# Four combinations of a weight matrix, made in sixteen slices between matmul pieces instead of in one stretch

## The chip, the cores and the metric

The kernel runs on one core of a Trainium2 chip. The time is what the device takes for one execution, in microseconds (us), as the median of the runs shown. The core's engines work side by side, each through its own list of instructions in order, and wait for each other through semaphores: TensorE (PE in the profile, its weight loads PEld), VectorE (DVE), ScalarE (ACT), GpSimd (POOL) and SyncE (SP), which here only starts transfers.

## The reference

A delta-rule attention over 4 batches of 8 heads (768 steps, heads of 48), and a feed-forward block on its output. All is float32.

```python
for t in range(S):
    y[:, :, t] = q_t @ state
    v_old = state applied to k_t                       # k normalized per head
    state = state + beta_t * outer(k_t, v_t - v_old)
x = y as (3072 tokens, 384)
h = x @ w_in                                           # w_in 384 x 2048
g = h * sigmoid(1.702 * h)
out = g @ w_out                                        # w_out 2048 x 384
```

## The kernel before, in words

**Units and pairs.** The sequence is cut into six chunks of 128 steps. A chunk of one batch is a unit, so there are 24 units, numbered 0 to 23, four per chunk. Two neighbouring units (256 tokens) are a pair, and the feed-forward block is done by pairs.

**The attention work of a unit.** The key tile KN of a unit is normalized (`normalize`, lines 296 to 310) in three steps: POOL squares it (`ksq`, line 300); DVE sums the squares (`ssq`) and POOL takes a power of them (`rn`, line 305); DVE adds a small number and takes the reciprocal, and POOL multiplies KN by it (line 309). Then PE transposes KN (`psT`), forms its Gram matrix (`psG`), and a transfer through DRAM puts the diagonal blocks into the tile NT. For every two units DVE inverts these blocks by some twenty pairs of a product `P` and a reduction (`invert`, line 427). Separately POOL masks a unit's score tile M by a select (line 578). There are seven KN buffers, KN0 to KN6; a buffer's next load is started from POOL's own list (line 94), once PE has read the buffer for the last time.

**The feed-forward block.** `hidden` (line 678) makes one pair's `x @ w_in` in sixteen pieces of three matmuls (`ph`; each matmul is two records in the profile), and ScalarE applies the activation into the tiles `gT`. For the first two pairs, `both_written` and `written` multiply `gT` by w_out as it stands (tile `po`). From the third pair on, `seven` (line 725) does the product over 2 x 2 blocks with seven products in place of eight. These need four combinations of the blocks W11, W12, W21, W22 of w_out, made once by `combined` (line 720): T1 = W12 - W11, T2 = W22 - T1, T3 = W22 - W12 (written over W12), T4 = W21 - T2. T1, T2 and T4 lie side by side in the scratch tile TW, 1536 columns each. The second pair's `gT` tiles for the upper half of w_out's rows lie in TW too, in columns 0 to 2047 (`late_g`), and columns 2048 and up hold a mask M and older tiles. So TW may be written only after PE's last products of the second pair that read those columns.

**The order.** `woven(n)` (line 910) writes out the work of step n: the attention steps of units n-1, n and n+1, the normalization of unit n+5, the inversion, and between them `spend`, which takes feed-forward pieces from a queue by a cost budget (`take`, line 833). `follow(n)` appends the next pair's `hidden` and `seven` to that queue. PE, DVE and ACT instructions go through a wrapper that keeps the written order. The POOL instructions of these steps (`ksq`, `rn`, the multiplication of KN, the select, the additions `add`, the loads of KN) don't: a scheduler places them in POOL's list. In this kernel the four additions of `combined` are emitted at the end of the second pair's `written`, by the small generator in the change below.

Of the kernel before, what the change touches and what calls it, by code (L numbers as in the profile page):

```python
# [18 lines left out]
def kernel(  # L19
# [32 lines left out]
    HB = 2  # L52
    NTH = HB * C
    FQ = 4
    GB = 6
    HF, HM = FC // 2, DM // 2
# [18 lines left out]
    units = [(c, b) for c in range(NC) for b in range(B)]  # L75
# [15 lines left out]
    def load(n, pairs, dma=nc.sync.dma_start):  # L91
        c, b = units[n]
        for dst, src in pairs:
            dma(  # L94
                out=place(dst, n)[:, :, 0:D],
                in_=src[b, :, c * C : (c + 1) * C, :].rearrange("h p d -> p h d"),
            )

    def load_values(n, dma=nc.sync.dma_start):
        c, b = units[n]  # L100
        V = io.tile([128, H, D], F32, tag="V", name="V", bufs=4)
        dma(
            out=V, in_=v[b, :, c * C : (c + 1) * C, :].rearrange("h p d -> p h d")
        )
        loaded[n] = V
# [183 lines left out]
    def fill(n):  # L289
        for _ in range(n):  # L290
            next(converting, None)
# [379 lines left out]
    add_, sub_ = ALU.add, ALU.subtract  # L671
    late_g = [TW[:, a : a + FQ * NTH].rearrange("p (f t) -> p f t", f=FQ) for a in (0, 1024)]

    def g_tile():

        return wk.tile([128, FQ, NTH], F32, tag="gT", name="gT", bufs=GB)

    def hidden(xT, gT, t, cost, sums=None, late=False):

        n = t.stop - t.start  # L680
        for f0 in range(0, FC, 2):
            if f0 // FQ == len(gT):
                gT.append(late_g[f0 // FQ - 2] if late and f0 >= FC // 2 else g_tile())
            ph = ps_moe.tile([128, 2, n], F32, tag="moe", name="ph")
            for u in range(2):
                f = f0 + u
                for j in range(KC):
                    pe.matmul(
                        ph[:, u], lhsT=w_in[:, j, f * 128 : (f + 1) * 128], rhs=xT[:, j, t],
                        start=(j == 0), stop=(j == KC - 1),  # L690
                    )
                if u == 0:
                    yield cost
            act.activation(
                gT[f0 // FQ][:, f0 % FQ : f0 % FQ + 2, t], ph, ACT.Gelu_apprx_sigmoid
            )
            if sums is not None and f0 + 2 in (3 * FQ, 4 * FQ):
                k = (f0 + 2) // FQ - 3
                if k == 0:
                    sums.append(g_tile())  # L700
                lo, hi, S1 = gT[k], gT[k + 2], half_of(sums[0], k)
                add(S1, lo[:, :, C:NTH], hi[:, :, C:NTH], add_)
                add(lo[:, :, C:NTH], lo[:, :, 0:C], lo[:, :, C:NTH], sub_)
            yield cost

    def half_of(t, k):

        return t.rearrange("p f (o t) -> p (f o) t", o=2)[:, k * FQ : (k + 1) * FQ]

    def add(o, a, b, op, engine=None):  # L710
        (engine or nc.gpsimd).tensor_tensor(o, a, b, op=op)  # L711
# [7 lines left out]

    def combined():  # L720

        for o, a, b in ((T1, W12, W11), (T2, W22, T1), (T3, W22, W12), (T4, W21, T2)):
            add(o, a, b, sub_)

    def seven(c, b0, gT, sums):

# [69 lines left out]
    def written(c, b0, gT):  # L796

        for i in range(HB):
            b = b0 + i
            po = ps_moe.tile([128, DM], F32, tag="moe", name="po")  # L800
            for f in range(FC):
                pe.matmul(
                    po, lhsT=gT[f // FQ][:, f % FQ, i * C : (i + 1) * C], rhs=w_out[:, f, :],
                    start=(f == 0), stop=(f == FC - 1),
                )
                if f % 2 == 1 and f < FC - 1:
                    yield 1.3
            o = wk.tile([128, DM], F32, tag="o", name="o")
            act.copy(o, po)
            nc.sync.dma_start(out=out[b * S + c * C : b * S + (c + 1) * C, :], in_=o)  # L810
            yield 1.3

    def both_written(c, gT):

        po = [ps_moe.tile([128, DM], F32, tag="moe", name="po") for _ in range(HB)]
        for n, f in enumerate(order):
            while ("out", f - f % 2 if 4 <= f < 8 else f) not in done:
                fill(1)
            fill(3)
            for i in range(HB):  # L820
                pe.matmul(
                    po[i], lhsT=gT[f // FQ][:, f % FQ, i * C : (i + 1) * C], rhs=w_out[:, f, :],
                    start=(n == 0), stop=(n == FC - 1),
                )
            if n < FC - 1:
                yield 1.3
        for i in range(HB):
            o = wk.tile([128, DM], F32, tag="o", name="o")
            act.copy(o, po[i])
            sync(out=out[i * S + c * C : i * S + (c + 1) * C, :], in_=o)  # L830
        yield 1.3
# [11 lines left out]
    def run(work):  # L843
        for _ in work:
            pass
# [5 lines left out]
    steps, xTs, inverting = {}, {}, iter(())  # L851
# [32 lines left out]
    def follow(n):  # L884

        if n + 3 < len(units):
            load(n + 3, ((QP, q),))
        m = n - 1 + len(KN)
        if m < len(units):
            load(m, ((KN, k),), nc.gpsimd.dma_start)  # L890
        if n - 1 + B < len(units):
            load_values(n - 1 + B)
        if n % HB == 0 and n > B:
            h = (n - 1) // HB
            gT, sums = [], []
            queue.append(hidden(xTs[h], gT, slice(0, NTH), 1.3, sums))
            queue.append(seven(*units[h * HB], gT, sums))
            xTs.pop(h)

# [10 lines left out]
    def woven(n, share):  # L910
# [36 lines left out]
        next(new_step(n + 2).scored, None)  # L947
        spend(share / 6)
        follow(n)

    queue = []
# [119 lines left out]
    gTs = [], []  # L1071
# [31 lines left out]
    while ffn:  # L1103
        feed()
    fill(10)
    def last_written():
        yield from written(*units[HB], gTs[1])
        combined()

    queue = [both_written(0, gTs[0]), last_written()]  # L1110
    for n in range(B - 1, len(units) + 1):
        woven(n, 19.5 if n > 6 else 10.4)
    run(take(1e9))
# [31 lines left out]
```

## Time and profile before

| | us |
|---|---|
| median of 3 runs | 823.84 |
| lowest and highest run | 815.86, 824.9 |
| span of the profiled execution | 813.5 |

What an execution takes beside its span isn't in the profile; the lowest run is 2.4 us above the span, the median 10.3.

| engine | busy us | share | instructions |
|---|---|---|---|
| PE | 748.9 | 92% | 8464 |
| DVE | 501.4 | 62% | 1029 |
| POOL | 249.4 | 31% | 210 |
| ACT | 238.5 | 29% | 523 |

| stretch, us from the start of the span | length | PE busy | granted clock of PE |
|---|---|---|---|
| 0 to 120 | 120.0 | 96.9 | 0.73 |
| 120 to 203 | 83.0 | 67.1 | 0.94 |
| 203 to 264 | 61.0 | 51.5 | 0.92 |
| 264 to 296 | 32.0 | 23.3 | 0.89 |
| 296 to 614 | 318.0 | 314.9 | 1.00 |
| 614 to 813.5 | 199.5 | 195.3 | 1.00 |

Times are counted from the start of the span. "Released" or "<-" names what an engine waited for last. The granted clock is the share of its full speed that PE was given. Nearly all instructions carry line 109, which is the wrapper's; they are told apart by their tiles, "out<-in".

### The profile page before, as it was taken

How to read it: one execution, taken by the hardware profiler on the slowest of the kernel's cores; microseconds unless marked ns; L12 is line 12 of the kernel's file. 1: busy time of each engine (PE TensorE's matmuls, PEld its weight loads, DVE VectorE, ACT ScalarE, POOL GpSimd, SP SyncE). 2: the span in 40 equal slices, each digit the busy share in tenths (PEclk: the TensorE clock that was granted, in tenths of full speed). 3: DMA queues.
4: the chain of work that ended last, by engine and by line, in shares of the span. 5: the costliest groups of instructions: out<-in, count | busy, mean ns of one | idle time of the engine just before them, and what ended most of it. 6: DMA issues, size and time to landing. Idle time of an engine off the chain costs nothing.

```text
span 813.5 us, 19675 instructions
## 1 busy us (share of the span) xinstructions
PE 748.9 (92%) x8464; PEld 636.4 (78%) x8464; DVE 501.4 (62%) x1029; ACT 238.5 (29%) x523; POOL 249.4 (31%) x210
## 2 busy tenths in 40 slices
PE   8678889777789779999999999999999999999998
PEld 6566668644456669889888898898898898998988
DVE  5797581998578667668767777786676681110000
ACT  3332263223323322242232232332422312312120
POOL 5011030011023826235254262282160330502213
PEclk9576599889799989999999999999999999999999
DMA  9945466244112410420421323224204102000000
GB/s 163 148 74 106 102 173 163 43 111 118 55 50 66 102 45 18 103 63 18 106 53 42 83 54 74 58 56 103 56 18 94 21 15 47 2 25 2 22 3 19
DMA packets 143654, 54.45 MB, mean 67 GB/s; under 512 B 113664, under 2 KB 138368, under 8 KB 143568
## 3 DMA queue, kind: packets, MB, share of 16 engines
q1 hardware_dynamic: 141936, 48.42, 27.0%
q0 software_dynamic: 1536, 4.52, 2.3%
q8 instruction: 66, 1.08, 0.6%
q10 hardware_dynamic: 96, 0.26, 0.1%
q14 instruction: 20, 0.16, 0.1%
HBM read 33.13 MB, written 18.87 MB: 64 GB/s over the span
## 4 chain that ended last, share of the span: by engine, by line
PE 70%; DVE 16%; DMA 4%; POOL 3%; issue 3%; SPq 2%; ACT 1%; DVEq 0%; POOLq 0%
PE ph L109 25%; PE po L109 24%; PE psY L109 6%; PE psU L109 5%; DVE P L109 4%; PE psQ L109 3%; DVE YB L109 3%; PE psT L109 2%; DVE TW L109 2%; PE psG L109 2%; SPq L109 2%; PE psR L109 2%; DVE NT L109 2%; DVE w_out L109 2%; POOL TW L711 1%
## 5 line engine op out<-in xcount | busy, mean ns | idle before, releaser
L109 PE MATMUL ph<-xT,w_in 128*128 128x256 f32 x1152 | 268.7, 390 | 0.0
L109 PEld LDWEIGHTS ph<-xT,w_in 128*128 128x128 f32 x1152 | 219.8, 194 | 33.3 <-DVE V L109 1.4
L109 PE MATMUL po<-w_out,gT 128*128 128x192 f32 (+1 forms) x736 | 152.8, 361 | 18.7 <-DVE w_out L109 11.0
L109 PEld LDWEIGHTS po<-w_out,gT 128*128 128x128 f32 x736 | 122.3, 193 | 37.2 <-DVE w_out L109 14.8
L711 POOL TENSOR_TENSOR gT<-gT 128x512 f32<-128x512 f32 x80 | 105.8, 1331 | 124.6 <-ACT gT L109 114.1
L109 DVE TENSOR_TENSOR V<-V,psR 64x384 f32<-64x384 f32 (+1 forms) x96 | 53.3, 556 | 134.7 <-PE psR L109 133.5
L109 DVE TENSOR_TENSOR P<-NT,YB 64x2 f32<-64x2 f32 (+9 forms) x200 | 98.4, 492 | 6.4
L109 ACT ACTIVATE gT<-ph 128x512 f32<-128x512 f32 x92 | 54.9, 596 | 152.9 <-PE ph L109 152.8
L109 PEld LDWEIGHTS psU<-V,XB 32*32 32x32 f32 x1536 | 61.6, 109 | 31.5 <-issue 16.5
L109 DVE TENSOR_REDUCE YB<-P 64x2 f32<-64x2 f32 (+9 forms) x200 | 81.8, 409 | 6.9
L109 PE MATMUL po<-TW,gT 128*128 128x192 f32 x480 | 83.0, 328 | 0.0
L109 ACT COPY US<-psU 32x384 f32<-32x384 f32 x92 | 43.2, 469 | 125.0 <-PE psR L109 115.4
L109 PE MATMUL psU<-V,XB 32*32 32x48 f32 x1536 | 73.0, 209 | 6.5 <-DVE V L109 4.8
L109 PEld LDWEIGHTS po<-TW,gT 128*128 128x128 f32 x480 | 77.9, 190 | 1.1 <-issue 0.3
L109 PE MATMUL psR<-US,G 32*32 32x48 f32 x2208 | 63.1, 207 | 0.6 <-ACT US L109 0.5
L578 POOL TENSOR_SCALAR_AFFINE_SELECT M<-M 128x1024 f32<-128x1024 f32 x19 | 23.6, 1245 | 123.5 <-DVE M L109 62.1
L109 DVE TENSOR_TENSOR o<-o,po 128x192 f32<-128x192 f32 x40 | 13.5, 351 | 75.8 <-PE po L109 75.3
L109 PEld LDWEIGHTS psR<-US,G 32*32 32x32 f32 x2208 | 53.5, 108 | 2.0 <-ACT US L109 1.1
L94 POOL DMA_DIRECT2D KN<-in_k_dram x15 | 14.4, 959 | 99.0 <-PE psY L109 99.0
L109 DVE TENSOR_TENSOR P<-NT 64x512 f32<-64x512 f32 (+7 forms) x50 | 43.0, 860 | 2.1
L109 PE MATMUL ps_warm<-ident 128*128 128x256 bf16 x176 | 31.5, 339 | 11.4 <-ACT G L109 6.5
L109 PE MATMUL psQ<-QS,kT 48*128 48x176 f32 (+1 forms) x368 | 35.5, 337 | 4.9 <-ACT QS L109 4.8
(110 smaller groups left out, 776.8 us busy)
## 6 DMA issues: line engine op xcount, KB each, us to landing
Nd<-G SPq DMA_DIRECT2D x20, 512.0 KB, 3.5
V<-in_v_dram SPq DMA_DIRECT2D x24, 192.0 KB, 3.2
out_dram<-o SPq DMA_DIRECT2D x24, 192.0 KB, 2.6
QP<-in_q_dram SPq DMA_DIRECT2D x22, 192.0 KB, 3.4
w_out<-in_moe_w_in_dram SPq DMA_DIRECT2D x18, 192.0 KB, 4.6
raw<-in_moe_w_out_dram SPq DMA_DIRECT2D x9, 384.0 KB, 4.0
NT<-Nd SPq DMA_DIRECT2D x24, 128.0 KB, 2.6
XB<-Yd SPq DMA_DIRECT2D x24, 128.0 KB, 3.1
```

The source lines that it names most:

```text
L94: dma(out=place(dst, n)[:, :, 0:D], in_=src[b, :, c * C : (c + 1) * C, :].rearrange("h p d -> p h d"),)
L109: return lambda *a, **kw: tc.keep_in_program_order(op(*a, **kw))
L578: (pool if self.n < B else nc.gpsimd).affine_select(out=self.M, in_=self.M, compare_op=ALU.is_gt, fill=0.0, base=0, pattern=[[0, H], [1, 1 ...
L711: (engine or nc.gpsimd).tensor_tensor(o, a, b, op=op)
```

## The change

The four subtractions of 1536 columns become sixteen of 384 (two of the eight row blocks at a time). `combined` is now a generator, and `beside_of` emits one slice after each piece of the third pair's `hidden`; the end of the second pair's `written` emits none.

```diff
     def combined():
 
+        n = 2
         for o, a, b in ((T1, W12, W11), (T2, W22, T1), (T3, W22, W12), (T4, W21, T2)):
-            add(o, a, b, sub_)
+            for f in range(0, HF, n):
+                add(o[:, f : f + n], a[:, f : f + n], b[:, f : f + n], sub_)
+                yield
+
+    def beside_of(work, other):
+
+        for cost in work:
+            next(other, None)
+            yield cost
+        run(other)
...
             gT, sums = [], []
-            queue.append(hidden(xTs[h], gT, slice(0, NTH), 1.3, sums))
+            work = hidden(xTs[h], gT, slice(0, NTH), 1.3, sums)
+            queue.append(beside_of(work, combined()) if h == HB else work)
             queue.append(seven(*units[h * HB], gT, sums))
...
-    def last_written():
-        yield from written(*units[HB], gTs[1])
-        combined()
-
-    queue = [both_written(0, gTs[0]), last_written()]
+    queue = [both_written(0, gTs[0]), written(*units[HB], gTs[1])]
```

In the built program the lists of PE, DVE, ACT and SP are in the same order as before. POOL's list differs in one place. In it, before the change: power of KN4, multiplication of KN4, load of KN5, square of KN5, T1, T3, T2, T4 (whole), select of M, power of KN5, multiplication of KN5. After it, slices counted 0 to 3 in each combination, with what POOL waits for before a slice where that is work of PE:

```
power of KN4
T1 slice 0   (PE: second unit's po product with row block 8)
T3 slice 0
multiplication of KN4
T1 slice 1   (PE: po, row block 10)
T3 slice 1
T1 slice 2   (PE: po, row block 11)
T3 slice 2
T2 slice 2   (PE: the psY products that read the mask in TW)
T4 slice 2
load of KN5  (as before: PE's last reading of KN5)
T1 slice 3   (PE: po, row block 13)
square of KN5 (as before: the load has landed)
T2 slice 3, T3 slice 3, T2 slice 0 (PE: po, row block 14), T4 slice 3,
T2 slice 1 (PE: po, row block 15), T4 slice 0, T4 slice 1
select of M
power of KN5
multiplication of KN5
```

## The prediction

> **What bounds the kernel now.** I read the forty slices first, then the chain of waits, then single engines where the chain leaves PE. PE is the bound: from 296 us on it is busy 510.1 of 517.5 us, so what moves PE's work at 296 earlier should move the end as much. Before that there are holes, and the combinations sit in one. The chain that ended last, from 264 us (start, duration, what):
>
> ```profile
> 267.27 3.45 POOL TW L711
> 270.79 3.43 POOL w_out L711
> 274.22 3.40 POOL TW L711
> 277.69 4.30 POOL TW L711
> 281.98 1.04 POOL M L578
> 283.03 1.64 POOL rn L305
> 284.67 3.44 issue
> 288.14 1.01 POOL KN L309
> ...
> 289.20 1.11 PE psT L109 x4
> ```
>
> The chain leaves PE for 22 us: four combinations, then what stands behind them in POOL's list, until KN5 is multiplied and PE may transpose it. PE alone shows the price (start, duration, tiles, idle before):
>
> ```profile
> 278.48 2.86 PE L109 MATMUL ph<-xT,w_in 128*128 128x256 f32 x12
> 289.20 1.11 PE L109 MATMUL psT<-ident,KN 128*128 128x128 f32 x4 [7.86 <-POOL KN L309]
> 290.11 5.65 PE L109 MATMUL ph<-xT,w_in 128*128 128x256 f32 x18
> ```
>
> Two units later the same 18 records (two to a matmul) take 4.05 us (from 348.71), and PE's transpose there waits for nothing. DVE tells why POOL's multiplication came so late:
>
> ```profile
> 274.23 4.46 DVE L109 TENSOR_TENSOR NT<-NT,bI 64x1024 f32<-64x1024 f32 x1 [4.61 <-DMA NT<-Nd]
> 278.72 3.28 DVE L109 TENSOR_TENSOR P<-NT,YB 64x2 f32<-64x2 f32 x1
> 282.04 0.15 DVE L109 TENSOR_REDUCE YB<-P 64x2 f32<-64x2 f32 x1
> 282.22 0.82 DVE L109 TENSOR_TENSOR P<-NT,YB 64x8 f32<-64x8 f32 x1
> ...
> 340.04 0.15 DVE L109 TENSOR_TENSOR P<-NT,YB 64x2 f32<-64x2 f32 x1
> ```
>
> The 64x2 product takes 0.15 us at 340 and 3.28 here: it ends at 282.0, as the fourth combination does. The NT product (1.22 us elsewhere, 330.14) ends 1.1 us after the third. So a DVE product of two SBUF tiles and a POOL operation exclude each other, whole operations at a time, and DVE lost 3.24 + 3.13 + 0.66 = 7.0 us before its reciprocal. Last, the granted clock (length, PE busy, PEld, DVE, ACT, POOL, clock, DMA):
>
> ```profile
> 282.00:283.00 1.00, 0.00 (x0) 0.00 (x0) 0.93 (x3) 0.00 (x0) 1.00 (x1) 1.00 0.00 0
> 286.00:287.00 1.00, 0.00 (x0) 0.00 (x0) 0.90 (x4) 0.00 (x0) 0.00 (x0) 0.76 0.00 0
> 292.00:293.00 1.00, 1.00 (x4) 0.82 (x3) 0.97 (x2) 0.00 (x0) 0.00 (x0) 0.50 0.00 0
> 294.00:295.00 1.00, 1.00 (x7) 0.87 (x6) 0.00 (x0) 0.50 (x1) 0.00 (x0) 1.00 0.00 0
> ```
>
> Idle since 281.3, PE falls to half speed near 286.5 (5.2 us later) and is back near 293.3.
>
> **The change, part by part.** *Price of a slice.* A quarter of a combination is 3.43 / 4 = 0.86 us; the 384-column square takes 0.82 alone and up to 1.10 beside DVE; three quarters of the 512-column addition (1.26) are 0.95. I take 0.9 and 0.05 between slices, with 0.82 and 1.27 as ends (the upper as if 384 columns cost what 512 do). Sixteen make 15.2 us, against 14.7 now, so the change saves no POOL work. It moves nine slices ahead of KN5's square; seven stay between it and the select.
>
> [...]
>
> *T1 and T3 slice 0, ahead of KN4's multiplication.* POOL is free at 253.37, but slice 0 waits for PE's product with block 8, the first half of four records from 253.93 in 1.45 us: 254.7. Two slices end at 256.6; KN4's multiplication began at 256.22, by DVE's reciprocal, and took 1.09 beside a DVE product. It now ends 0.2 to 1.1 us later; I take 0.5. PE's transpose of KN4 waits for it (1.99 us of idle), and all of PE behind it, so this is a loss on the path.
>
> *Six slices from T1 slice 1 to T4 slice 2, ahead of KN5's load.* They wait for PE at 259.1 and later and end near 264.8. POOL was idle there: the load waited 5.20 us for PE until 262.52. The load now starts 2.3 us later. Queued behind it are T1 slice 3, which fits while it lands, and the square, 3.8 us after the load's start: 268.6 to 270.5 instead of 266.31. The square's reader on DVE is followed by the NT product, which waits for a transfer until 274.23 now (274.7 with the 0.5), so this costs nothing; without that cover it would cost up to 4 us. DVE's own products there collide with slices; the NT-from-YB product (265.40) feeds the XB transfer, for which PE waited 0.80 us at 277.68. I add up to 1 us: PE's twelve `ph` records end at 282.2 instead of 281.34.
>
> *Seven slices after the square.* From 270.3, at 0.95, they would end at 277.0. The NT product comes between (1.22) and one small product: 278.4. Select 1.09, power 1.67: 281.2. DVE: NT product 275.1 to 276.3, then three products that each wait for a POOL operation, the third out at 279.7; the other six with their reductions take 3.3 (341.20 to 344.50): 283.2. V, sum and reciprocal 1.1, multiplication 0.83: PE's transpose at 285.1 instead of 289.20, **4.1 us earlier**. Lower end: with DVE never held, 274.7, then 1.22 for the NT product, 4.5 for the nine pairs (340.01 to 344.50) and 2.0 for the rest make 282.4, just behind PE's own work (6.8 earlier). Upper end: slices of 1.27 put the last seven 2.6 later: 287.6 (1.6 earlier).
>
> *The clock.* PE would be idle 282.2 to 285.1, 2.9 us. After 2.99 us of idle (up to 236.39) the clock stayed 1.00 in the stretch behind; after 4.10 us (up to 173.48) it was 0.63. So the half-speed stretch should go: transpose to the end of the 18 records takes 6.56 us here and 4.49 at 348.27, **2.1 us** won. If the idle stays over 4, nothing is won.
>
> [...]
>
> *Sum.* 4.1 + 2.1 = 6.2 us: span 807.3 and, against the median of the runs shown, 817.6. The lowest run less 6.2 would be 809.7. What is late next in that stretch is DVE's chain to the reciprocal; behind 290, DVE has 3.56 us of idle before it is needed at 296.66, which moves with PE. T1 to T4 are first read at 308.97 or later, long after either version makes them.
>
> **The rivals.** *Hidden wholly:* DVE is hardly held, and PE finds KN5 ready at 282.4. 6.8 + 2.1 = 8.9 us, 814.9. For it: POOL now idles 5.20 us before KN5's load and 2.83 behind it, and the slices fill this; against it: seven remain behind the square.
>
> *Half a gain:* slices near 1.27 us, or DVE losing each turn, keep the transpose at 287.6 and the clock dips as now: 1.6 us, 822.2. For it: the additions beside DVE reach 1.74 us; against it: the 0.82 rows.
>
> *Slower:* the new waits on PE at the head of POOL's list. T1 slice 0 stands before KN4's multiplication, and T2 slice 2 before KN5's load. If KN4 is 1.1 us late and the square lands so late that all seven slices meet DVE's nine products turn by turn (9 x 0.95 = 8.6 us on top of 274.7 + 1.22 + 4.5 + 2.0 = 282.4, so 291.0), PE's transpose is 1.8 us later than now, 825.6. It decides when the square ends after about 274 (270.3 expected). Against it: seven slices can't hold nine products.
>
> That the slices don't move is excluded by the built order.
>
> **How the numbers follow.** The forecast has 0.58, hidden wholly 0.20, half a gain 0.15, slower 0.07. The runs of before spread over 1.1%, so about 1% is what a measurement can tell from no change. The forecast is 0.75% and passes 1% (8.2 us) by that spread in four of ten cases, hidden wholly in six: 0.23 + 0.12, about 0.36 for faster. Slower by over 1% needs most of the last rival, with the spread: 0.06. Within: 0.58. The range reaches from 810 (lowest run less 6.2) to 823 (half a gain, with 1 us).
>
> **What would show it.** PE's idle before KN5's transpose falls from 7.86 to about 3 us; the clock stays 1.00 from 282 to 295; no DVE product there takes over 1.5 us except NT's at about 2.1; KN4's transpose comes at 257.9, KN5's load near 265. I am wrong if the slices take over 1.2 us each, if the idle stays over 5 us, or if a new hole opens between 258 and 282, the XB wait above all.

## The result, and the profile after

| | before | after |
|---|---|---|
| median of 20 runs each, us | 817.97 | 811.61 |
| lowest and highest | 811.71, 824.9 | 806.27, 819.11 |
| ratio of the times, 95% interval | | 0.9918 [0.9894, 0.9942] |
| span of the profiled execution | 813.5 | 806.6 |

The change wins 0.8%, and 811.61 us lies in the predicted range; the forecast of 6.2 us less is met by the runs (818.0 to 811.6). The forecast as a time, 817.6, was 6 us too high, since the three runs from which it was counted have a median of 823.84 and the twenty here 817.97. The profiled spans differ by 6.9. (Medians, here and below, count all runs; the ratios leave disturbed ones out.) The terms behind these totals did not all come true, though, as the same views show.

First the chain of waits of the kernel after, through the same stretch (start, duration, what):

```profile
268.72 0.96 POOL w_out L711
269.67 5.75 POOL TW L711 x5
275.42 1.05 POOL M L578
276.48 1.63 POOL rn L305
278.11 3.45 issue
281.60 1.01 POOL KN L309
...
282.66 0.74 PE psT L109 x4
```

The chain has the same shape: combinations, select, power, a wait, KN5's multiplication, PE's transpose. But seven slices now stand where four whole combinations stood. PE alone (start, duration, tiles, idle before):

```profile
255.06 0.66 PE L109 MATMUL psT<-ident,KN 128*128 128x128 f32 x4 [2.79 <-POOL KN L309]
255.55 2.52 PE L109 MATMUL po<-w_out,TW 128*128 128x384 f32 x4
...
276.95 2.86 PE L109 MATMUL ph<-xT,w_in 128*128 128x256 f32 x12
...
282.66 0.74 PE L109 MATMUL psT<-ident,KN 128*128 128x128 f32 x4 [2.85 <-POOL KN L309]
283.19 5.70 PE L109 MATMUL ph<-xT,w_in 128*128 128x256 f32 x18
```

PE waits 2.85 us before KN5's transpose instead of 7.86. But the eighteen `ph` records behind it still take 5.70 us, as they did before (5.65), and not 4.05. New is the second line: the four `po` records behind KN4's transpose take 2.52 us. In the kernel before they took 1.46, behind a wait of 1.99:

```profile
257.37 0.66 PE L109 MATMUL psT<-ident,KN 128*128 128x128 f32 x4 [1.99 <-POOL KN L309]
257.87 1.46 PE L109 MATMUL po<-w_out,TW 128*128 128x384 f32 x4
```

DVE of the kernel after in the same stretch:

```profile
272.67 1.90 DVE L109 TENSOR_TENSOR NT<-NT,bI 64x1024 f32<-64x1024 f32 x1 [3.75 <-DMA NT<-Nd]
274.60 0.84 DVE L109 TENSOR_TENSOR P<-NT,YB 64x2 f32<-64x2 f32 x1
275.48 0.15 DVE L109 TENSOR_REDUCE YB<-P 64x2 f32<-64x2 f32 x1
275.67 0.83 DVE L109 TENSOR_TENSOR P<-NT,YB 64x8 f32<-64x8 f32 x1
...
276.72 0.17 DVE L109 TENSOR_TENSOR P<-NT,YB 64x18 f32<-64x18 f32 x1
```

The NT product has gone from 4.46 to 1.90 us and the 64x2 product from 3.28 to 0.84; it still ends with POOL's last slice (275.42), and the last slow one, 64x8 at 0.83 us, with the select (276.47), but these operations are short. The granted clock (length, PE busy, PEld, DVE, ACT, POOL, clock, DMA):

```profile
256.00:257.00 1.00, 1.00 (x3) 0.62 (x2) 0.95 (x2) 0.35 (x1) 0.12 (x1) 0.50 0.00 0
258.00:259.00 1.00, 1.00 (x53) 0.99 (x56) 0.96 (x2) 0.00 (x0) 1.00 (x1) 0.50 0.00 0
282.00:283.00 1.00, 0.34 (x3) 0.34 (x4) 0.93 (x3) 0.00 (x0) 0.60 (x1) 1.00 0.00 0
284.00:285.00 1.00, 1.00 (x4) 0.78 (x3) 0.93 (x3) 0.03 (x1) 0.00 (x0) 0.50 0.00 0
287.00:288.00 1.00, 1.00 (x6) 0.90 (x5) 0.00 (x0) 0.37 (x1) 0.00 (x0) 1.00 0.00 0
```

PE runs at half speed twice, from 255.80 to 259.21 and from 283.10 to 286.51: behind its wait of 2.79 us for KN4, which the profile before doesn't have, and behind that of 2.85 us for KN5.

To set spans side by side I cut each profile at four instructions of PE that all kernels have: the last `po` records that read `gT` ahead of KN4's transpose (A), KN4's transpose, KN5's transpose, and the `psQ` records just ahead of the first products of `seven` (D). Lengths in us:

| kernel | start to A | A to KN4 | KN4 to KN5 | KN5 to D | D to end | A to end |
|---|---|---|---|---|---|---|
| before | 252.53 | 4.84 | 31.83 | 18.37 | 505.93 | 560.97 |
| after | 249.42 | 5.64 | 27.60 | 18.04 | 505.90 | 557.18 |

Up to A both kernels run the same instructions, so 3.1 us of the 6.9 between the two spans are chance: the granted clock of that stretch was 0.83 in the one profile and 0.86 in the other. What the change does itself in these two profiles is in the last column: 3.8 us. In all ten experiments A came between 248 and 262 us. That part scatters, and a span alone says little about a change of this size.

### The profile page after: what moved, and what is told of

It is laid out like the page before. It is cut to its first block, busy times and chain, and to the rows that moved or that the text cites. A ratio compares the mean times of both kernels' runs of the same rounds, so it can differ in the third digit from the quotient of the medians.

```text
span 806.6 us, 19689 instructions
## 1 busy us (share of the span) xinstructions
PE 745.0 (92%) x8464; PEld 633.7 (79%) x8464; DVE 499.7 (62%) x1029; ACT 238.6 (30%) x523; POOL 251.3 (31%) x222
## 3 DMA queue, kind: packets, MB, share of 16 engines
q0 software_dynamic: 1536, 4.52, 2.3%
## 4 chain that ended last, share of the span: by engine, by line
PE 67%; DVE 15%; issue 5%; DMA 5%; POOL 4%; SPq 2%; ACT 1%; DVEq 0%; POOLq 0%
PE ph L109 25%; PE po L109 23%; PE psY L109 5%; PE psU L109 5%; DVE P L109 4%; PE psQ L109 3%; DVE YB L109 3%; SPq L109 2%; DVE TW L109 2%; PE psR L109 2%; PE psT L109 2%; DVE w_out L109 2%; POOL TW L711 2%; DVE NT L109 1%; PE psG L109 1%
## 5 line engine op out<-in xcount | busy, mean ns | idle before, releaser
L109 PE MATMUL po<-w_out,gT 128*128 128x192 f32 (+1 forms) x736 | 150.3, 357 | 18.5 <-DVE w_out L109 10.8
```

Of the source, the lines that this page charges most:

```text
L109: return lambda *a, **kw: tc.keep_in_program_order(op(*a, **kw))
```

## The experiments

The prediction's theory was: the four whole additions sit in POOL's list ahead of KN5's multiplication, they hold DVE besides, and slices that move ahead of KN5's square undo both; the rest of the gain is a clock that no longer falls. Each kernel was profiled once; its stretches are in the table. The diffs are against the kernel after, but for e9's, which is against e7.

| kernel | start to A | A to KN4 | KN4 to KN5 | KN5 to D | D to end | A to end |
|---|---|---|---|---|---|---|
| e1 no combinations | 248.48 | 4.85 | 24.30 | 16.36 | 505.91 | 551.42 |
| e2 whole, behind the power | 249.71 | 4.85 | 38.56 | 18.03 | 505.95 | 567.39 |
| e3 slices in written order | 253.07 | 4.84 | 29.22 | 19.35 | 513.82 | 567.23 |
| e4 clock kept up | 253.47 | 5.64 | 26.82 | 16.36 | 505.91 | 554.73 |
| e5 whole, between pieces | 257.88 | 4.84 | 31.56 | 18.42 | 506.00 | 560.82 |
| e6 slices, one stretch | 256.92 | 5.64 | 27.56 | 18.05 | 505.93 | 557.18 |
| e7 early and late slices | 262.39 | 4.85 | 27.64 | 16.36 | 510.56 | 559.41 |
| e8 the same, clock kept up | 254.25 | 4.85 | 24.65 | 16.37 | 510.58 | 556.45 |
| e9 two in between | 253.73 | 4.85 | 25.26 | 16.36 | 506.20 | 552.67 |
| e10 the same, clock kept up | 251.96 | 4.84 | 25.27 | 16.36 | 506.17 | 552.64 |

**e1: what the combinations cost at all.** The four combinations are left out, so the products from the third pair on read tiles that hold other data.

```diff
-            queue.append(beside_of(work, combined()) if h == HB else work)
+            queue.append(work)
```

> The four combinations are left out (T1 to T4 hold what lay there before, so the output differs); all else as in the changed kernel. It is the floor: what the combinations cost at all. Theory (the cost was PE's hole before KN5's transpose, and the half-speed stretch behind it): POOL multiplies KN5 near 280, PE waits for nothing there, KN4's transpose is not later than before; 6.8 + 2.1 = 8.9 us under the kernel before, ratio 0.989, some 2.5 us under the changed kernel. Rival (half of the gain of the changed kernel's profile, 3.1 of 6.9 us, lies before 251 us, where no instruction differs, so it is chance): no more than 6 us under the kernel before, ratio 0.993 or higher.

Measured: median 806.23 us of 6 runs, ratio 0.9843 [0.9788, 0.9898]. PE of this kernel at KN5's transpose:

```profile
277.63 0.66 PE L109 MATMUL psT<-ident,KN 128*128 128x128 f32 x4 [0.81 <-POOL KN L309]
278.12 4.05 PE L109 MATMUL ph<-xT,w_in 128*128 128x256 f32 x18
```

PE waits 0.81 us and keeps its clock; A to end is 9.6 us below the kernel before. That is all there is to win here. The theory had 8.9. It also had this floor some 2.5 us under the kernel after; it is 5.8 under it (5.4 by the medians), and 2.45 of that is the clock which the kernel after loses twice (e4, below).

**e2: four whole additions behind the power.** They are pinned to POOL and thereby keep their written place, behind the power and ahead of KN5's multiplication.

```diff
-        n = 2
+        n = HF
...
-                add(o[:, f : f + n], a[:, f : f + n], b[:, f : f + n], sub_)
+                add(o[:, f : f + n], a[:, f : f + n], b[:, f : f + n], sub_, pool)
```

> The four combinations whole (1536 columns), but held in the written order, so that they stand in POOL's list behind the select and KN5's power and ahead of KN5's multiplication. It tells POOL's list apart from DVE being held. Theory (a POOL operation and a DVE product of two SBUF tiles exclude each other for whole operations): NT's product and the first two small ones each wait for a combination, DVE's reciprocal comes near 290.8, PE's transpose of KN5 near 291.8 on the clock of the profile before, 2.6 us later than there; ratio 1.003. Rival (only the place in POOL's list counts): the combinations end near 284.8, the transpose comes near 285.7, 3.5 us earlier, and ratio 0.995 or lower.

Measured: median 822.06 of 12, ratio 1.0053 [1.0017, 1.0088]. DVE of this kernel, in the stretch in which POOL makes the combinations (272.76 to 287.32):

```profile
273.87 3.40 DVE L109 TENSOR_TENSOR NT<-NT,bI 64x1024 f32<-64x1024 f32 x1 [3.97 <-DMA NT<-Nd]
277.31 3.29 DVE L109 TENSOR_TENSOR P<-NT,YB 64x2 f32<-64x2 f32 x1
...
280.81 3.16 DVE L109 TENSOR_TENSOR P<-NT,YB 64x8 f32<-64x8 f32 x1
...
284.20 3.16 DVE L109 TENSOR_TENSOR P<-NT,YB 64x18 f32<-64x18 f32 x1
```

Four DVE products, four additions, one for one, where the theory had three products held; where nothing is on POOL (e1) the same four take 1.22, 0.16, 0.17 and 0.18 us. KN5's multiplication then waited for DVE's reciprocal, 4.74 us after POOL was done with everything else, and PE's transpose waited 12.12. In this order POOL's list delays nothing that DVE waits for, and PE still waits longer than before: whole additions cost through DVE, and not by their place in the list alone. Counted from KN4's, KN5's transpose came 6.7 us later than before, and not 2.6: beside the fourth product, the clock fell behind KN4's transpose in this profile (0.56 from 254.6 to 262.4).

**e3: slices in the written order.** Sixteen slices pinned to POOL, begun from the third piece on, so that most come behind KN5's multiplication.

```diff
-                add(o[:, f : f + n], a[:, f : f + n], b[:, f : f + n], sub_)
+                add(o[:, f : f + n], a[:, f : f + n], b[:, f : f + n], sub_, pool)
...
-        for cost in work:
-            next(other, None)
+        for i, cost in enumerate(work):
+            if i >= 2:
+                next(other, None)
```

> Sixteen slices as in the change, but held in the written order and begun two pieces later, so that none stands ahead of KN4's multiplication, KN5's load or KN5's power; four (T1) stand between KN5's power and its multiplication, the others behind it. Theory: KN4's transpose is as early as before, DVE is held by at most two slices, PE's wait before KN5's transpose is under 1 us; about 8 us under the kernel before, ratio 0.990, a little better than the changed kernel. Rival (the slices then come too late for the third pair's products and POOL's other work): PE waits 2 us or more between 295 and 320, and the ratio is 0.993 or higher.

Measured: median 821.72 of 12, ratio 1.0007 [0.9964, 1.0049]. The wait before KN5's transpose is 2.90 us, where under 1 was expected: the four slices ahead of KN5's multiplication held three DVE products (2.04, 0.84 and 0.74 us), not two at most, and the clock fell behind KN4 (0.58 from 257.9 to 265.7) and KN5 (the transpose takes 1.11 us, and 0.66 in e1). What gain there is, is given back one unit later. POOL of this kernel:

```profile
312.00 1.48 POOL L109 TENSOR_TENSOR TW<-w_out,TW 128x384 f32<-128x384 f32 x1
313.44 1.31 POOL L578 TENSOR_SCALAR_AFFINE_SELECT M<-M 128x1024 f32<-128x1024 f32 x1
314.73 1.83 POOL L305 TENSOR_TENSOR rn<-ssq,half 128x8 f32<-128x8 f32 x1
316.54 1.94 POOL L109 TENSOR_TENSOR TW<-w_out,TW 128x384 f32<-128x384 f32 x2
318.45 5.29 POOL L711 TENSOR_TENSOR gT<-gT 128x512 f32<-128x512 f32 x3
323.70 0.83 POOL L309 TENSOR_TENSOR KN<-KN,rn 128x384 f32<-128x384 f32 x1
```

Late slices push KN6's multiplication to 323.70, and PE waits 6.00 us for it at 324.58. D to end is 7.9 us longer than before. The rival held, with the wait some microseconds later than it said: what is moved off KN5's path must not land on KN6's.

**e4: the clock kept up.** Twenty products of constants, whose result nobody reads, ahead of KN4's and KN5's transposes, in time in which PE waits anyway.

```diff
         c, b = units[n]
+        if n in (11, 12):
+            ps = ps_seq.tile([128, 256], F32, tag="seq", name="ps_warm")
+            for _ in range(20):
+                pe.matmul(ps, lhsT=ones[:, 0:128], rhs=ones, start=True, stop=True)
         turn(n)
```

> The changed kernel with twenty small matmuls of constants (128x256, bfloat16, result unused) on PE ahead of KN4's and of KN5's transpose, where PE otherwise waits 2.8 us each. Theory (in the changed kernel's profile PE ran at half speed for some 3.4 us behind each of these two waits; each cost about 1.6 to 2.1 us): the clock stays 1.00 from 250 to 290 and the time is 3 to 4 us under the changed kernel, ratio to before near 0.987. Rival (whether the clock drops after so short a wait differs from run to run, or the lost speed is not on the path): under 1.5 us below the changed kernel, ratio 0.990 or higher; if the matmuls delay the transposes, slower than the changed kernel.

Measured: median 809.53 of 6, ratio 0.9885 [0.9842, 0.9929]. PE of this kernel:

```profile
256.15 2.35 PE L109 MATMUL ps_warm<-ident 128*128 128x256 bf16 x20
259.11 0.66 PE L109 MATMUL psT<-ident,KN 128*128 128x128 f32 x4 [0.62 <-POOL KN L309]
...
285.93 0.65 PE L109 MATMUL psT<-ident,KN 128*128 128x128 f32 x4 [1.25 <-POOL KN L309]
286.42 4.05 PE L109 MATMUL ph<-xT,w_in 128*128 128x256 f32 x18
```

The clock is 1.00 behind both transposes (256 to 263, 286.4 to 290), and the `ph` records take 4.05 us again. A to end falls by 2.45 us, 0.78 of them between KN4 and KN5 and 1.68 behind KN5; somewhat less than the 3 to 4 expected. The extra products delay nothing: A to KN4 is 5.64 with and without them.

**e5 and e6: slicing or interleaving.** e5 spreads four whole additions between the pieces, e6 makes sixteen slices in one stretch at the end of `written`.

```diff
-        n = 2
+        n = HF
```

> The four combinations whole, each emitted behind a piece of the third pair's x @ w_in, as the change places its slices. Every engine's list, waits included, is the same as in the kernel before. Theory (the place where the additions are written does nothing, since the scheduler puts them where their inputs allow; the smaller size does it all): ratio 1.000, within 0.3%, PE's wait before KN5's transpose 7 to 8 us. Rival (the interleaving with the pieces is what helps): ratio 0.992 as with the changed kernel. It also gives a second profile of the order before: theory of the clock lottery (a wait of 2.0 us before KN4's transpose is followed by half speed in some executions and not in others) allows either.

```diff
-            queue.append(beside_of(work, combined()) if h == HB else work)
+            queue.append(work)
...
+    def last_written():
+        yield from written(*units[HB], gTs[1])
+        run(combined())
```

> Sixteen slices, all emitted in one stretch at the end of the second pair's output, where the kernel before has its four whole combinations. Every engine's list, waits included, is the same as in the changed kernel. Theory: ratio 0.992, as the changed kernel (0.9918), PE's wait before KN5's transpose 2.5 to 3.5 us. Rival (the interleaving is what helps): ratio 1.000.

Measured: e5 819.66 of 12, ratio 1.0024 [0.9987, 1.0061], and every engine's list is that of before, waits included. e6 812.8 of 12, ratio 0.995 [0.9912, 0.9987], and every list is that of after. The stretches agree with before and after to 0.3 us each, and to 0.2 from A to the end. So the interleaving, which gives the change its name, does nothing: a scheduler places an unpinned addition by what it reads and writes. All of the effect comes from the smaller slices. T1's slice 1 needs only the `po` products that read its own columns, while whole T1 needs all of them.

**e7 to e10: a better place.** Slices ahead of KN4's multiplication (after) and ahead of KN6's load (e3) cost time. e7 leaves seven slices to the scheduler, which fit between KN4's multiplication and KN5's square, and pins nine behind KN5's multiplication, two for each piece from the seventh on.

```diff
+    EARLY = (1, 1), (3, 1), (1, 2), (3, 2), (2, 2), (4, 2), (1, 3)
+    LATE = (1, 0), (3, 0), (3, 3), (2, 0), (2, 1), (2, 3), (4, 0), (4, 1), (4, 3)
...
-        for cost in work:
-            next(other, None)
+        for i, cost in enumerate(work):
+            for _ in range(2 if i >= 6 else 0):
+                next(other, None)
...
```

> The sixteen slices in two groups. Seven (all slices 1 and 2 but two, and T1 slice 3) stand where they do in the changed kernel, between KN4's multiplication and KN5's square; the other nine are held in the written order behind KN5's multiplication, where POOL waits 7.8 us for KN6's load in the run without combinations. None stands ahead of KN4's multiplication, none between KN5's square and its multiplication. Theory: KN4's transpose is not delayed (PE waits 2.0 us, not 2.8), PE's wait before KN5's transpose is about 1 us as without the combinations (0.81), nothing new is late behind it; from PE's product before KN4's wait to the end some 9 us less than before (9.6 without combinations), ratio to before 0.985 to 0.988, better than the changed kernel. Rival (the nine late slices hold DVE or KN6's load, so that a wait of 2 us or more appears between 290 and 315): ratio 0.990 or higher.

e8 adds sixteen of e4's products ahead of KN4's transpose (`n == 11`).

> The kernel with early and late slices, and sixteen small matmuls of constants on PE ahead of KN4's transpose (result unused), where PE waits 2.0 us. Theory (a wait of 2.0 us there is followed by half speed in some executions, costing some 2 us): the clock stays 1.00 from 250 to 262 and the median is 0.5 to 2 us under the kernel with early and late slices alone. Rival (no speed is lost there as a rule): no difference, or slower by up to 0.5 us.

Measured: e7 818.05 of 12, ratio 0.997 [0.9918, 1.0023]; e8 812.02 of 12, ratio 0.9949 [0.9911, 0.9987]. KN5's transpose now waits 0.82 us, as in e1, but D to end is 4.6 us longer. POOL of e8 shows why:

```profile
287.19 6.12 POOL L109 TENSOR_TENSOR TW<-w_out,TW 128x384 f32<-128x384 f32 x6
293.26 0.96 POOL L94 DMA_DIRECT2D KN<-in_k_dram  x1
299.00 0.82 POOL L300 TENSOR_TENSOR ksq<-KN 128x384 f32<-128x384 f32 x1 [4.78 <-DMA KN<-in_k_dram]
```

KN6's load is started from POOL's list and stands behind nine slices; POOL then idles 4.78 us until it has landed, KN6 is late, and PE waits 2.52 us before its transpose at 314.62 (2.50 in e7). So e7's rival held, through KN6's load, and A to end is 1.6 us below before where some 9 were expected. Counted from KN5's transpose, the load starts 1.8 us later than in e1, and it also takes 5.7 us from its start to the square behind it, where e10, below, has 3.5. Why it takes longer isn't shown. Between e7 and e8 only the clock behind KN4's transpose differs from A on (0.58 from 267.2 to 275 in e7; the four `po` records there take 2.12 us in e7 and 1.46 in e8): KN4 to KN5 is 27.64 against 24.65. The medians differ by 6.0, twice as much; the rest isn't explained.

e9 puts two of the nine slices between KN5's power and its multiplication, where POOL idled 8.22 us in e8; e10 is e9 with e8's sixteen products.

```diff
-            for _ in range(2 if i >= 6 else 0):
+            for _ in range(2 if i >= 6 else i // 4):
```

> As the kernel with early and late slices, but two of the nine late ones (T1 and T3, slice 0) stand between KN5's power and its multiplication, where POOL waits for DVE; seven stay behind the multiplication. Theory (the nine late slices started KN6's load 2 us late, and that alone made PE's wait of 2.5 us before KN6's transpose, 4.7 us from the third pair's first products to the end): KN6's load starts within 0.3 us of PE's last reading, that wait is gone, the stretch from the third pair's first products to the end is 505.9 us again; NT's product waits up to 1 us more. From KN4's transpose to the end 546 to 551 us (before 556.1, changed kernel 551.5), the spread by whether the clock drops behind KN4's transpose; ratio 0.987 to 0.991. Rival (the four additions of gT, delayed with the slices, make the wait): it stays above 1.5 us and the ratio is 0.993 or higher.

> The same with sixteen small matmuls of constants ahead of KN4's transpose (result unused). Theory: no half speed behind KN4's transpose in any execution, from KN4's transpose to the end about 547 us (before 556.1), ratio to before 0.986 to 0.990, at least as fast as the changed kernel. Rival (the rest of the half-speed stretches and the early part hide it): same as the changed kernel, 0.991 to 0.995.

Measured: e9 810.61 of 12, ratio 0.9915 [0.9883, 0.9948]; e10 805.48 of 6, ratio 0.9854 [0.9803, 0.9906], the best of the kernels that make the combinations. POOL of e10:

```profile
273.25 1.00 POOL L109 TENSOR_TENSOR w_out<-w_out 128x384 f32<-128x384 f32 x1
281.01 1.00 POOL L309 TENSOR_TENSOR KN<-KN,rn 128x384 f32<-128x384 f32 x1 [6.76 <-DVE rn L109]
281.98 1.16 POOL L109 TENSOR_TENSOR w_out<-w_out 128x384 f32<-128x384 f32 x1
283.10 6.60 POOL L109 TENSOR_TENSOR TW<-w_out,TW 128x384 f32<-128x384 f32 x6
289.81 0.96 POOL L94 DMA_DIRECT2D KN<-in_k_dram  x1
293.30 0.82 POOL L300 TENSOR_TENSOR ksq<-KN 128x384 f32<-128x384 f32 x1 [2.53 <-DMA KN<-in_k_dram]
```

KN6's load starts 7.7 us behind KN5's transpose, as in e1; the wait for it is 2.53 us, and D to end is back to within 0.3 of before. A to end is 552.6, 1.2 us above e1, which makes no combinations at all. e9 has the same stretches, because its clock happened to hold in the profile (1.00 from 258.6 to 263). How e10's runs come out some 5 us below e9's is explained only in part by that chance; the rest would have to lie in the scatter up to A, which six runs don't settle.

## Why the prediction was right, and where it was not

**What the combinations cost.** The reading held: POOL's list and DVE's held products together keep KN5 from PE. e1 gives 9.6 us for it, and e2 shows the holding in an order in which POOL's list delays nothing for DVE.

**KN4's multiplication, 0.5 us later (0.2 to 1.1).** Measured 0.80 (5.64 against 4.84 from A). The wait that it lengthens, from 1.99 to 2.79 us, had a second price that I did not count: half speed behind KN4's transpose, 0.78 us on the path by e4.

**KN5's transpose 4.1 us earlier.** From A it is 3.43 earlier, and 4.21 in e4, where the clock stays up. Slices, turns and DVE's chain came as worked out: three held products at 1.90, 0.84 and 0.83 us against "no DVE product there takes over 1.5 us except NT's at about 2.1". The charge of up to 1 us for the wait for XB was not needed; no new hole opened there.

**The clock, 2.1 us.** This is the step that failed in the profile: "So the half-speed stretch should go". KN5's transpose to the end gained 0.36 us instead. I had read from two waits, 2.99 us without and 4.10 with a fall, that 2.9 is safe. One wait that did no harm is no bound: the shorter waits of 2.79 and 2.85 us both lost the clock. In the clock's records of these two profiles, counted in steps of 3.41 us (last section), at most 1.91 of the 2.99 us lay in one step, and all of the 2.85. In e4 the stretch from KN5's transpose to the end gains 2.03 us, so the size was right and the condition was not.

**The sum.** With the clock kept up, e4 has 6.24 us less than before from A to the end, where 6.2 were predicted for the change alone. The change itself has 3.8 in the profiles. Its runs nevertheless show more: pooling all runs with before's lists (before in every round, and e5; 107 runs, mean 818.4) and with after's (after and e6; 32 runs, 812.2), 6.1 ± 1.5 us. A part may be that the order of before, too, loses its clock behind KN4's transpose in some executions: three of the seven profiles whose wait there is 2.00 us show that, and e7 against e8 prices it at 3.0 us on the path, which makes an estimate of 3/7 x 3.0 = 1.3 us and a difference of 5.1. Neither before's nor e5's profile was such an execution, so this is an argument and not shown. The order of after may in turn keep its clock in some executions; both of its profiles (after and e6) lost it behind both waits, and e4 prices the two at 2.45 us. This isn't shown either. That the median fell by the predicted 6.2 us is in part luck: the change won that much without the step that was to give a third of it.

**The price of a slice, 0.9 with 0.82 and 1.27 as ends.** The operations of the addition's line in the kernel after (count: shortest/median/longest ns, first and last start, shape):

```profile
L711 POOL TENSOR_TENSOR TW<-w_out,TW x8: 995/999/1978, 261.2 to 273.4; 128x384 f32<-128x384 f32 x8
L711 POOL TENSOR_TENSOR TW<-w_out x4: 989/992/1008, 251.7 to 264.2; 128x384 f32<-128x384 f32 x4
```

A slice takes 0.99 us undisturbed. Sixteen are 15.8 us where four whole additions of 3.43 are 13.7: 2.1 us for twelve more instructions, 0.18 each. So a slice cost more here than a quarter of a whole addition, and the quarter (0.86) and the squares (0.82), on which the 0.9 rested, were too low for it. It cost little here, because the nine early slices, but for the two ahead of KN4's multiplication, lie in POOL's idle time.

**The rivals.** None came. "Hidden wholly" failed because seven slices still stand ahead of the select; e10 shows that it could be had with other places. "Half a gain" had its clock right and its cause wrong. "Slower" needed the square after 274; it came at 266.93, which is 270.0 on the clock of the profile before. That the slices move was rightly read from the built lists, but what moves them is their size and not, as the change's words have it, the pieces between which they are emitted (e5, e6).

## What to carry to other kernels

Where a scheduler places instructions by what they read and write, splitting a long one may move it and emitting it elsewhere may not; compare the built lists of each half of such a change before timing it. An operation that holds another engine should go where both idle, and the next unit's load and multiplication in the same list have to be counted, or the gain returns one unit later. A wait of PE of 2.00 us on the path cost the clock behind it here in three profiles of seven; with matmuls of constants in the wait it stayed 1.00 (e4 from 256 to 263, e10 from 256.8 to 261).

## What the runs showed of the hardware

**The clock fell after short waits, but not always.** Behind a wait of 1.99 or 2.00 us for KN4, with the same instructions up to there, the clock held in four profiles (1.00 in before, e1, e5, e9) and fell in three (0.56 in e2, 0.58 in e3 and e7). One row each, of before and of e3, columns as in the clock's view above:

```profile
257.40:262.00 4.60, 4.60 (x120) 3.55 (x120) 4.20 (x6) 1.26 (x3) 0.00 (x0) 1.00 0.02 4
```

```profile
257.90:265.70 7.80, 7.79 (x122) 5.91 (x122) 4.23 (x6) 1.33 (x3) 0.00 (x0) 0.58 0.01 2
```

The same 120 or so matmuls take 4.6 us at a clock of 1.00 and 7.8 at 0.58. The times of PE's records show other falls. Behind waits of 2.79 us for KN4 (after, e6) the four `po` records take 2.52 and 2.42 us, and 1.46 in before. Behind 2.85 and 2.33 us before KN5 (after, e6) the eighteen `ph` records take 5.70 and 5.74, and 4.05 in e1; behind 2.90 (e3) the transpose takes 1.11, and 0.66 in e1. Behind 2.52 us before KN6 (e8) 24 `po` records take 5.59, and 4.07 in before, which has no wait there; behind 2.50 (e7) the thirteen from 326.22 take 3.96 and the thirteen from 329.55 take 2.42. Behind a wait of 2.98 or 2.99 us for KN3, which every profile has, the four `po` records take 1.46 us in ten of the twelve, 2.60 in e7 and 1.92 in e10. So between 2.0 and 3.0 us the length of a wait did not decide by itself here.

The clock's records show more. In the profiles of before and of after all changes of the clock lie whole multiples of 3.413 us apart, to within 0.002; the half-speed stretches of after at 255.80 and 283.10 are one such step each, that of before at 286.51 is two. Here are two neighbouring steps of before, and two stretches of the same length in e3, around the wait for KN4:

```profile
255.79:259.21 3.42, 1.84 (x8) 1.07 (x8) 3.28 (x6) 0.60 (x1) 1.09 (x1) 1.00 0.00 0
259.21:262.62 3.41, 3.41 (x121) 3.08 (x122) 2.78 (x6) 0.73 (x2) 0.10 (x1) 1.00 0.02 5
```

```profile
255.69:259.10 3.41, 1.41 (x8) 0.92 (x8) 3.24 (x7) 0.49 (x1) 1.10 (x1) 1.00 0.00 0
259.10:262.52 3.42, 3.42 (x79) 2.23 (x81) 2.47 (x4) 0.58 (x2) 0.00 (x0) 0.50 0.02 5
```

In before a boundary of the steps falls within the wait, PE is idle for 1.58 us of the first stretch, and the second runs at full speed. In e3 the wait lies in one stretch, PE is idle for 2.00 us of it, and the next runs at half. From 225 us to 790 in before and after, three steps at full speed were followed by half speed, with PE idle for 3.41 us of the one in before and for 2.68 and 2.85 us of the two in after; the other 325, with 1.91 us or less, were not. Ahead of 225 us, in before, a step with 0.80 us of idle PE (85.13 to 88.54) was followed by half speed, and one with 1.94 (197.77 to 201.19) was not. So idle time does not tell it all; what else counts there isn't shown.

**POOL's select held DVE's products too, its power did not.** DVE's 64x8 product took 0.83 us beside the select of M (275.42 to 276.47 in the kernel after) and 0.17 in e1. The 64x2 product of 0.15 us at 340.04 in before ran beside POOL's power (338.91 to 341.54), so what the prediction says of a POOL operation is shown here for the additions and the select alone.
